# Normalized x of chunks 1 to 3 turned by VectorE instead of TensorE, between two tiles of 8 KB, with x loaded sooner

## The chip, the cores and the metric

The kernel runs on one core of one Trainium2 chip. The core has a matrix engine (TensorE, PE in the profile), a vector engine (VectorE, DVE), a scalar engine (ScalarE, ACT), a general engine (GpSimd, POOL) and a queue engine (SyncE, SP) that here issues DMAs. The metric is the time of one execution on the device in microseconds. The kernel before takes 844.69 us (median of three runs, 844.31 to 852.22).

## The reference

The input x has 2048 tokens of 512 values, all arithmetic is in fp32. One normalized copy of x feeds two branches, whose product is added to x:

```
xn = (x - mean) / sqrt(var + 1e-5)              # per token
qkv = xn @ wqkv                                 # 512 -> 3 x 32 heads x 16
p = softmax(q k^T * 16**-0.5, keys 0..255 behind the query)
s = (p v, heads side by side) @ wo
b = (silu(xn @ w_gate) * (xn @ w_up)) @ w_down  # hidden width 1792
out = x + s * silu(b)
```

A matrix product on TensorE sums over the partitions. So xn, which is loaded with tokens on the partitions, is needed turned: its 512 values on the partitions (four pieces k of 128) and tokens along the columns.

## The kernel before

**Chunks and units.** The tokens go in four chunks of 512. For each chunk TensorE runs dense units: projections to q and k (`Proj`, tiles "a"), gate and up (`GateUp`, "g" and "u"), values ("vp"), down ("d"), and the output projection of the chunk before ("s"). All of them go through line 619. For accuracy every operand is a sum of a high part and a low part, and a product is three matmuls: high x high, high x low, low x high. Names ending in h and l are these parts: xh, xl of the turned x, wh, wl of the weights. ScalarE rounds the high part, and another engine subtracts it to get the low one.

**Two halves.** The 128 rows of the array are used as two halves of 64 rows. A unit's sum runs first over the rows of the lower half (r = 0), and, some steps later, over those of the upper half (r = 1), into the same bank of PSUM. While the upper half still works on one unit, the lower half is on the next. Between the two stands a hand-over: a small copy on VectorE (tile "ho", line 616) that reads the bank after the lower half's last matmul. Four banks serve the dense units and four serve attention.

**Attention.** 32 units of four heads (eight per chunk). For each, scores are made once for the row maximum (b, line 1347; jk on VectorE, line 1355) and once transposed for the exponentials (c, line 1475; p on ScalarE), then probabilities times values (pv, line 1523). Every unit's maxima are turned by four small VectorE transposes (mr, line 1377). These short matmuls are placed between the dense ones. Queries, keys and results pass through DRAM.

**Normalizing and turning x.** `load_x` (line 259) fetches four tiles of 128 tokens by 512 values, takes mean and variance on VectorE, the inverse root partly on GpSimd, and scales in place (two tiles by VectorE, two by GpSimd). `xt_turn` (line 628) then turns one piece k: four tiles times two halves make eight TensorE transposes (xp, line 639) into two banks, ScalarE copies each bank to xh (line 657), VectorE subtracts to get xl (line 654). Four visits per chunk. Chunk 0 is turned in a similar way from its own code at the start, and once more by `xt_turn`.

**What sets the order.** All instructions are written out by a planner that runs while the program is built. It keeps a clock for each half of TensorE and each engine, with assumed costs. Work for the other engines waits in a queue per engine with an urgency; the most urgent that can go is emitted as soon as the engine is free in the plan. On TensorE, the half with the earlier clock gets the next matmul; a half whose inputs, weights or bank are not there by the plan gets none, and the other half goes on alone:

```
able = [r for r in range(2) if times[r] is not None and times[r] <= max(clock[r], now[0])]
...
r = min(able, key=lambda r: clock[r])
```

Attention and turning are started by due times, in units of `PACE` of dense work, less `LEAD`. The load of chunk c is due at 8c - `LXD`, its turning at 8c - `XTD`. So a change of a constant can move every instruction. The emitted order is fixed; on the chip each engine works through its instructions in that order and waits where a semaphore isn't there.

**Tiles.** 14 tiles of 128 x 512 values (`slots`) serve x, the evacuated q and k, hidden values, attention results and the x that is added at the end. `take` gets one and `give` returns it. `SURE` is the margin after which a tile that GpSimd reads counts as free, `MG` the urgency of the weights' low parts.

Of the kernel before, what the change touches and what calls it, by code (L numbers as in the profile page):

```python
# [9 lines left out]
F32 = mybir.dt.float32  # L10
F32R = mybir.dt.float32r
BF16 = mybir.dt.bfloat16
AF = mybir.ActivationFunctionType
ALU = mybir.AluOpType
# [3 lines left out]
P = 128  # L18
# [6 lines left out]
KC = D // P  # L25
# [14 lines left out]
NSL = 14  # L40
# [2 lines left out]
OPEN = 11  # L43
PRESS = 1.0
MS = 5.5
MG = 4.0
SPARE = 2
LAG = 7
MW = 80
SURE = 0.598  # L50
MTC = 0.85
CO = 1.075
MSG = 0.0
QKG = 1.0
LXD = 5.0
XTD = 3.5
WSL = 0.778
VDUE = 0.75

# [2 lines left out]
PRIO = -0.5  # L62
MM = 0.2315
PACE = 17.6
LEAD = 1.04
OUT = 2.4
STEP = 0.05
LAND = 3.5
# [4 lines left out]
def tile_window_attention_swiglu_gate(  # L73
# [12 lines left out]
    nc = tc.nc  # L86
    ctx.enter_context(tc.manual_schedule())
    pers = ctx.enter_context(tc.tile_pool(name="pers", bufs=1))
# [17 lines left out]
    def f32(ap):  # L106
        return ap.bitcast(F32)
# [38 lines left out]
    def timer(t, fn, *a):  # L146
        seq[0] += 1
        heapq.heappush(timers, (t, seq[0], fn, a))
# [20 lines left out]
                    again = True  # L169


    slots = [f"sl{i}" for i in range(NSL)]
    held = {}

    def take(name, shape=(P, 512), dtype=F32):
        assert slots, name
        tag = slots.pop(0)
        t = pers.tile(list(shape), dtype, name=name, tag=tag, bufs=1)
        held[id(t)] = (t, tag)
        return t  # L180

    def give(t):
        slots.append(held.pop(id(t))[1])

    def room(n):
        return lambda: len(slots) >= n
# [72 lines left out]
    def load_x(c):  # L259
        mv = pers.tile([P, 4, 2], F32, name=f"mv{c}", tag="mv")  # L260
        ve, rs, tm, nm = (
            pers.tile([P, 4], F32, name=f"{n}{c}", tag=n) for n in ("ve", "rs", "tm", "nm")
        )
        left = [4]


        def stats(i):
            st = sb(f"st{c}_{i}", [P, 6], F32, "st", 2)
            nc.vector.bn_stats(st, xt[c, i])
            nc.vector.bn_aggr(mv[:, i, :], st)  # L270

        small, se = nc.gpsimd, "G"

        def eps():
            small.tensor_scalar(ve, mv[:, :, 1], EPS, None, op0=ALU.add)
            small.tensor_scalar(nm, mv[:, :, 0], -1.0, None, op0=ALU.mult)

        def roots(r=rs):

            i32 = mybir.dt.int32  # L280
            nc.vector.tensor_scalar(tm.bitcast(i32), ve.bitcast(i32), 1, None, op0=ALU.logical_shift_right)
            nc.vector.tensor_scalar(  # L282
                r.bitcast(i32), tm.bitcast(i32), -1, 0x5F3759DF, op0=ALU.mult, op1=ALU.add
            )

        def newton():
            for _ in range(3):
                small.tensor_tensor(tm, rs, rs, op=ALU.mult)
                small.tensor_tensor(tm, tm, ve, op=ALU.mult)
                small.tensor_scalar(tm, tm, -0.5, 1.5, op0=ALU.mult, op1=ALU.add)  # L290
                small.tensor_tensor(rs, tm, rs, op=ALU.mult)

        def scale(i):
            (nc.gpsimd if i % 2 else nc.vector).tensor_scalar(
                xt[c, i], xt[c, i], nm[:, i : i + 1], rs[:, i : i + 1], op0=ALU.add, op1=ALU.mult
            )

        sl = 3.0

        def fetch(i):  # L300
            xt[c, i] = take(f"xt{c}_{i}")
            move(xt[c, i], x[c * TC + i * P : c * TC + (i + 1) * P, :])

        def after_stats(t):
            left[0] -= 1
            if left[0] == 0:
                do(se, t, 0.25, eps, after_eps, sl)

        def after_eps(t):
            do("V", t, 0.3, roots, after_rec, sl)  # L310

        def after_rec(t):
            do(se, t, 2.4, newton, after_newton, sl)

        def after_newton(t):
            for i in range(4):
                e = "G" if i % 2 else "V"
                do(e, t, 1.1 if e == "G" else 0.55, lambda i=i: scale(i), lambda t, i=i: scaled(t, i), sl + 0.3 * i)

        def scaled(t, i):  # L320
            normed[c, i] = t

        for i in range(4):
            dma(now[0], lambda i=i: fetch(i), lambda t, i=i: do("V", t, 0.8, lambda: stats(i), after_stats, sl),
                slack=0.1 * i, can=room(5 - i + SPARE))

    turns = {}
    cready = {}
# [299 lines left out]
    def xt_turn(c, k):  # L628
        left = [2]
        for r in range(2):  # L630
            pb, tag = bank(rb_free, f"xp{c}_{k}_{r}")
            src = pb[:, :256].rearrange("p (t n) -> p t n", n=R)
            hi, lo = (
                xn[c % 2][s][:, k, :].rearrange("p (t r n) -> p t r n", r=2, n=R)[:, :, r, :]
                for s in range(2)
            )

            def go(t, r=r, pb=pb):
                nc.tensor.matmul(  # L639
                    pb[:, R * t : R * t + R], xt[c, t][half(r), k * P : (k + 1) * P],  # L640
                    ident[half(r), half(r)], is_transpose=True, start=True, stop=True,
                )

            def done(t, tag=tag):
                rb_free[tag] = t
                left[0] -= 1
                if left[0] == 0:
                    xready[c, k] = t
                    if k == KC - 1:
                        for i in range(4):  # L650
                            give(xt.pop((c, i)))

            def low(src=src, hi=hi, lo=lo):
                nc.vector.tensor_tensor(lo, src, f32(hi), op=ALU.subtract)

            def finished(t, src=src, hi=hi, low=low, done=done):
                do("S", t, 0.3, lambda: nc.scalar.activation(hi, src, AF.Copy),
                   lambda t: do("V", t, 0.35, low, done, 0.3), 0.3)

            for t in range(4):  # L660
                extra[r].append((128, lambda t=t, go=go: go(t), finished if t == 3 else None))

    PAIRS = ((0, 0), (0, 1), (1, 0))

# [921 lines left out]
    def plan_attention():  # L1586
        for u in range(NU):
            c = u // NG
            if u:
                marks.append((u - 1 + 0.3, load_qk, (u,)))  # L1590
            for n in range(8):
                streams[0].append((u + 0.02 + 0.1 * n, max_ready, max_pair, (u, n // 4, n % 4)))
            ne = 3
            for n in range(2 * ne):
                streams[1].append((u + CO + 0.13 * n, prob_ready, prob_pair, (u, n // 2, n % 2)))
            streams[1].append((u + 1.89, pv_ready, pv_visit, (u,)))
        for c in range(NCH):
            if c:
                marks.append((8 * c - LXD, load_x, (c,)))
            for k in range(KC):  # L1600
                due = 8 * c - XTD + 0.25 * k if c else -9.0
                streams[2].append((due, xt_ready, xt_turn, (c, k)))
        for s in streams:
            s.reverse()
        marks.sort(key=lambda m: -m[0])
# [259 lines left out]
```

## Time and profile before

| | before |
|---|---|
| median of three runs | 844.69 us |
| the profiled execution | 844.67 us |
| its span | 842.6 us |
| granted clock of TensorE | 0.999 |
| TensorE busy | 834.6 us (99%) |
| VectorE busy | 525.5 us (62%) |
| ScalarE busy | 488.4 us (58%) |
| GpSimd busy | 629.6 us (75%) |

The span runs from the first to the last instruction of the program; the execution's time is 2.07 us longer. PE is the matmuls, PEld the loading of their stationary operand, which overlaps them. Matmuls of the two halves run side by side and are pipelined: one of 512 columns shows about 0.39 us, and the pace is read from the distance of the starts. In the lists of groups, a row has the line, engine, operation, tiles (out<-in), shapes, count, then busy time in us and mean ns of one, then the idle time before them and what ended it. In the lists of waits, a row has who waited for whom, the us in total, the number of times and the longest. The chain of waits is the work that ended last, followed back from the end.

### The profile page before, as it was taken

To read this page: it belongs to the slowest core of one execution; us is meant where nothing else is said; L and a number is where in the kernel's file an instruction comes from. 1 tells how busy PE (TensorE), PEld (TensorE's weight loads), DVE (VectorE), ACT (ScalarE), POOL (GpSimd) and SP (SyncE) were. 2 spreads that over 40 slices of the span, in tenths; PEclk is the share of its full clock that TensorE was granted. 3 is DMA by queue.
4 is the path that set the end of the run, shared out by engine and by line. 5 is a ranking of instruction groups with operands and counts; after the bars stand their busy time and mean duration, and the time that the engine had idled before them with its cause. 6 is when DMAs were issued, how large, how long until landed. Compare 5 with 4: busy or idle time off the path is not lost.

```text
span 842.6 us, 26272 instructions
## 1 busy us (share of the span) xinstructions
PE 834.6 (99%) x9962; PEld 752.8 (89%) x9962; DVE 525.5 (62%) x1772; ACT 488.4 (58%) x950; POOL 629.6 (75%) x887
## 2 busy tenths in 40 slices
PE   8999999999999999999999999999999999999997
PEld 8999978988889999888988999889888889989887
DVE  4247786766756757667646976666646676645235
ACT  6545656665665566564666657655467565556531
POOL 6567695878867888677977897867688877888771
PEclk9999999999999999999999999999999999999999
DMA  6586866876678966467768968664878576764442
GB/s 171 159 211 146 198 138 156 185 180 162 160 192 198 266 163 160 117 173 169 169 157 208 230 150 193 150 168 117 203 176 210 113 195 178 173 154 103 115 107 73
DMA packets 67143, 139.98 MB, mean 166 GB/s; under 512 B 14710, under 2 KB 17654, under 8 KB 67016
## 3 DMA queue, kind: packets, MB, share of 16 engines
q1 hardware_dynamic: 66552, 137.64, 67.0%
q8 instruction: 79, 1.29, 0.7%
q10 hardware_dynamic: 464, 0.66, 0.3%
q14 instruction: 48, 0.39, 0.2%
HBM read 107.68 MB, written 29.62 MB: 163 GB/s over the span
## 4 chain that ended last, share of the span: by engine, by line
PE 97%; DVE 1%; DMA 1%; issue 0%; POOL 0%; DVEq 0%; SPq 0%; POOLq 0%
PE u L619 20%; PE d L619 19%; PE g L619 19%; PE a L619 9%; PE pv L1523 8%; PE c L1475 6%; PE s L619 6%; PE vp L619 6%; PE b L1347 4%; DMA xt<-x 1%; PE xp L639 0%; PE xp L457 0%; DVE jk L1355 0%; DVE rs L282 0%; DVE s L1196 0%
## 5 line engine op out<-in xcount | busy, mean ns | idle before, releaser
L579 POOL TENSOR_TENSOR wl<-wr,wh 128x512 fp32r<-128x512 f32 (+1 forms) x239 | 305.4, 1291 | 63.2 <-ACT wh L574 61.0
L1355 DVE CUSTOM_DVE_ANT_0 jk<-b,maskb 128x384 bf16<-128x384 f32 (+2 forms) x512 | 271.2, 530 | 93.2 <-PE b L1347 45.2
L1435 ACT ACTIVATE p<-c 128x512 f32<-128x512 f32 (+2 forms) x384 | 196.3, 572 | 77.9 <-PE c L1475 72.6
L619 PE MATMUL d<-wh,hh 64*128 64x512 f32 x896 | 227.8, 393 | 0.0
L574 ACT ACTIVATE wh<-wr 128x512 fp32r<-128x512 f32 (+1 forms) x239 | 145.1, 627 | 34.8 <-PE d L619 13.8
L619 PE MATMUL g<-xh,wh 64*128 64x512 f32 x448 | 152.9, 393 | 0.0
L619 PE MATMUL g<-xh,wl 64*128 64x512 f32 x448 | 152.8, 393 | 0.0
L619 PE MATMUL u<-xh,wl 64*128 64x512 f32 x448 | 152.1, 392 | 0.0
L619 PE MATMUL u<-xl,wh 64*128 64x512 f32 x448 | 152.1, 392 | 0.0
L619 PE MATMUL g<-xl,wh 64*128 64x512 f32 x448 | 151.9, 393 | 0.0
L619 PE MATMUL u<-xh,wh 64*128 64x512 f32 x448 | 151.8, 393 | 0.0
L619 PE MATMUL d<-wl,hh 64*128 64x512 f32 x448 | 145.7, 392 | 0.0
L619 PEld LDWEIGHTS d<-wh,hh 64*128 64x128 f32 x896 | 136.1, 185 | 6.2
L1447 POOL TENSOR_SCALAR_AFFINE_SELECT p<-p 128x256 f32<-128x256 f32 x256 | 102.4, 412 | 47.1 <-ACT p L1435 46.5
L1347 PE MATMUL b<-k,q 48*128 48x384 f32 (+2 forms) x512 | 111.1, 329 | 0.4 <-DVE m L1355 0.4
L774 POOL TENSOR_TENSOR hh<-h,hh 128x512 fp32r<-128x512 f32 x56 | 72.6, 1296 | 46.8 <-ACT hh L770 44.6
L1451 POOL TENSOR_SCALAR_AFFINE_SELECT p<-p 128x256 f32<-128x256 f32 x224 | 91.7, 411 | 17.8 <-ACT p L1435 16.1
L619 PE MATMUL a<-xh,wh 64*128 64x512 f32 x256 | 93.9, 392 | 0.0
L1475 PE MATMUL c<-q,k 49*128 49x128 f32 (+2 forms) x704 | 93.8, 299 | 0.0
L619 PE MATMUL a<-xl,wh 64*128 64x512 f32 x256 | 93.0, 392 | 0.0
L619 PE MATMUL a<-xh,wl 64*128 64x512 f32 x256 | 93.0, 392 | 0.0
L1475 PEld LDWEIGHTS c<-q,k 49*128 49x128 f32 x704 | 82.9, 186 | 5.1 <-DVE m L1355 0.2
(116 smaller groups left out, 1884.7 us busy)
## 6 DMA issues: line engine op xcount, KB each, us to landing
wr<-wgu SPq DMA_DIRECT2D x112, 256.0 KB
wr<-wdn SPq DMA_DIRECT2D x48, 256.0 KB
k<-qkd SPq DMA_DIRECT2D x48, 192.0 KB
wr<-wqk SPq DMA_DIRECT2D x32, 256.0 KB
qkd<-qkh SPq DMA_DIRECT2D x32, 256.0 KB
qkd<-qkl SPq DMA_DIRECT2D x32, 256.0 KB
q<-qkd SPq DMA_DIRECT2D x64, 128.0 KB
od<-ev SPq DMA_DIRECT2D x32, 256.0 KB
```

Of the source, the lines that this page charges most:

```text
L574: nc.scalar.activation(wtile[j, h][0][pr, a - 512 * h : b - 512 * h], raw[pr, a:b], AF.Copy)
L579: nc.gpsimd.tensor_tensor(lo, raw[pr, a:b], f32(hi), op=ALU.subtract)
L619: return nc.tensor.matmul(pb, a, b, start=first, stop=last, skip_group_check=True)
L774: nc.gpsimd.tensor_tensor(hl[:, 1, :], self.h, f32(hl[:, 0, :]), op=ALU.subtract)
L1347: nc.tensor.matmul(pb[:, :n], qs[u % 3][r : r + 48, p, qb * P : (qb + 1) * P], ks[u % 3][r : r + 48, p, lo : lo + n], start=True, stop=True,)
L1355: nc.vector.tensor_tensor_reduce(junk[:, :n], pb[:, :n], maskb[:, 3 * P - n :], 1.0, -3.0e38, ALU.add, ALU.max, m[:, col : col + 1],)
L1435: nc.scalar.activation(t[:, h, :], pc[:, :n], AF.Exp, scale=DH ** -0.5)
L1447: nc.gpsimd.affine_select(s, s, [[0, 2], [1, P]], ALU.is_ge, 0.0, base=0, channel_multiplier=-1)
L1451: nc.gpsimd.affine_select(s, s, [[0, 2], [-1, P]], ALU.is_gt, 0.0, base=0, channel_multiplier=1)
L1475: nc.tensor.matmul(pc[:, at0 : at0 + w], ks[u % 3][r : r + 49, p, k0 : k0 + P], qs[u % 3][r : r + 49, p, qb * P : qb * P + w], start=(i == ...
L1523: nc.tensor.matmul(pbs[r][0][32 * j : 32 * j + 32, q0:q1], vt[half(r), (4 * c + kb) % VT, VW * (4 * g + j) : VW * (4 * g + j) + 32], t[hal ...
```

## The change

The turning of chunks 1 to 3 leaves TensorE. x is loaded into one tile of 128 x 4 x 512 values (`wides[0]`, 8 KB per partition), each token tile in a fourth of it. After scaling, 16 instructions on VectorE turn it into a second such tile (`wides[1]`). One instruction takes 32 partitions (a block b of tokens) and the columns of one group f of values, 512 columns in all, turns its blocks of 32 x 32 and writes to 32 partitions. When all 16 are done, ScalarE copies each of four pieces k to xh, and GpSimd subtracts to get xl. Before, the subtraction was VectorE's, and the copies and subtractions went by half pieces from PSUM.

The two tiles are eight of the 14 tiles of `slots`: while a chunk doesn't need them, their fourths are given out as ordinary tiles, after the six others. `hold_wide` collects the four fourths before the load, or before the turning; `give_wide` returns them. Constants of the planner change as well: loads and turning are due sooner, `LEAD` shifts all due times, `SURE` is shorter, the `SPARE` tile kept back is one instead of two, and `MG` grows. Chunk 0 stays as it was.

```diff
-MG = 4.0
-SPARE = 2
+MG = 4.572
+SPARE = 1
...
-SURE = 0.598
+SURE = 0.243
...
-LXD = 5.0
-XTD = 3.5
+LXD = 5.8
+XSL = 0.5
+XDS = 1.0
+XDD = 3.3
+XDU = 1.5
+XTD = 4.4
...
-LEAD = 1.04
+LEAD = 1.173
...
-    slots = [f"sl{i}" for i in range(NSL)]
+    slots = [f"sl{i}" for i in range(NSL - 8)]
+    wides = [pers.tile([P, 4, 512], F32, name=f"wide{i}") for i in range(2)]
+    wide = wides[0]
+    slots += range(8)
...
-            xt[c, i] = take(f"xt{c}_{i}")
+            xt[c, i] = wide[:, i]
...
+    def hold_wide(n, c, then):
+        for i in range(4 * n, 4 * n + 4):
+            if i in slots:
+                slots.remove(i)
+                wide_held[n].append(i)
+        if len(wide_held[n]) == 4:
+            then(c)
+        else:
+            timer(now[0] + 0.3, hold_wide, n, c, then)
...
+    def x_wait(c):
+        if any((c, t) not in normed for t in range(4)):
+            timer(now[0] + 0.3, x_wait, c)
+            return
+        hold_wide(1, c, x_blocks)
+
+    def x_blocks(c):
+        left = [16, KC]
+
+        def blocks(b, f):
+            q = slice(32 * b, 32 * b + 32)
+            src = wide[q].rearrange("q t (k f d) -> q f t k d", f=4, d=32)[:, f]
+            dst = wides[1][32 * f : 32 * f + 32].rearrange("d k (t b q) -> d b t k q", b=4, q=32)[:, b]
+            nc.vector.transpose(dst, src)
+
+        def turned(at):
+            left[0] -= 1
+            if left[0] == 0:
+                timer(at, give_wide, 0)
+                for k in range(KC):
+                    do("S", at, 0.52, lambda k=k: high(k), lambda t, k=k: after_high(t, k), XSL + 0.3 * k, lambda: c in x_free)
+
+        def high(k):
+            nc.scalar.activation(xn[c % 2][0][:, k, :], wides[1][:, k], AF.Copy)
+
+        def low(k):
+            nc.gpsimd.tensor_tensor(xn[c % 2][1][:, k, :], wides[1][:, k], f32(xn[c % 2][0][:, k, :]), op=ALU.subtract)
...
+        for n in range(16):
+            do("V", max(now[0], at), 0.72, lambda n=n: blocks(n // 4, n % 4), turned,
+               lambda n=n: now[0] + n * 0.01 + (XDS if work[0] / PACE - LEAD < 8 * c - XDD else -XDU))
...
-                marks.append((8 * c - LXD, load_x, (c,)))
-            for k in range(KC):
-                due = 8 * c - XTD + 0.25 * k if c else -9.0
-                streams[2].append((due, xt_ready, xt_turn, (c, k)))
+                marks.append((8 * c - LXD, hold_wide, (0, c, load_x)))
+                marks.append((8 * c - XTD, x_wait, (c,)))
+            for k in range(KC if not c else 0):
+                streams[2].append((-9.0, xt_ready, xt_turn, (c, k)))
```

In the rows of the order below, as in the profile, a number follows each name. Units are named by chunk and place: u2_5 is up, chunk 2, hidden block 5; d2_0_1 is down, chunk 2, first quarter, token tile 1. Line 619 of before is line 651 after, 616 is 648, 1355 is 1426. A row of the two halves can be told by its unit: at the places shown, the lower half is one unit or more ahead.

More of the change, by code (lines that the diff above doesn't have):

```diff
@@ L177, in take @@
         tag = slots.pop(0)
-        t = pers.tile(list(shape), dtype, name=name, tag=tag, bufs=1)
+        if isinstance(tag, int):
+            t = wides[tag // 4][:, tag % 4]
+            if len(shape) == 3:
+                t = t.rearrange("p (a n) -> p a n", a=shape[1])
+            elif shape[1] < 512:
+                t = t[:, : shape[1]]
+            t = t if dtype == F32 else t.bitcast(dtype)
+        else:
+            t = pers.tile(list(shape), dtype, name=name, tag=tag, bufs=1)
         held[id(t)] = (t, tag)
@@ L182, in give @@
     def give(t):
-        slots.append(held.pop(id(t))[1])
+        tag = held.pop(id(t))[1]
+        slots.insert(len(slots) if isinstance(tag, int) else sum(not isinstance(o, int) for o in slots), tag)
     def room(n):
@@ L324, in load_x, with give_wide @@
             dma(now[0], lambda i=i: fetch(i), lambda t, i=i: do("V", t, 0.8, lambda: stats(i), after_stats, sl),
-                slack=0.1 * i, can=room(5 - i + SPARE))
+                slack=0.1 * i)
+    wide_held = [[], []]
+    def hold_wide(n, c, then):
[5 more added lines that the diff above has]
+            then(c)
+        else:
+            timer(now[0] + 0.3, hold_wide, n, c, then)
+    def give_wide(n):
+        slots.extend(wide_held[n])
+        wide_held[n].clear()
     turns = {}
@@ L661, in xt_turn, with after_high @@
                 extra[r].append((128, lambda t=t, go=go: go(t), finished if t == 3 else None))
+    def x_wait(c):
[20 more added lines that the diff above has]
+            nc.gpsimd.tensor_tensor(xn[c % 2][1][:, k, :], wides[1][:, k], f32(xn[c % 2][0][:, k, :]), op=ALU.subtract)
+            left[1] -= 1
+            if left[1] == 0:
+                timer(free_at["G"] + SURE, give_wide, 1)
+        def after_high(t, k):
+            do("G", t, 1.24, lambda: low(k), lambda t: xready.__setitem__((c, k), t), XSL + 0.3 * k)
+        at = max(normed[c, t] for t in range(4))
+        for n in range(16):
+            do("V", max(now[0], at), 0.72, lambda n=n: blocks(n // 4, n % 4), turned,
+               lambda n=n: now[0] + n * 0.01 + (XDS if work[0] / PACE - LEAD < 8 * c - XDD else -XDU))
     PAIRS = ((0, 0), (0, 1), (1, 0))
```

## The prediction

> **What bounds the kernel now.** I read the page first: span, busy shares, the chain that ended last.
>
> ```profile
> span 842.6 us, 26272 instructions
> ...
> PE 834.6 (99%) x9962; PEld 752.8 (89%) x9962; DVE 525.5 (62%) x1772; ACT 488.4 (58%) x950; POOL 629.6 (75%) x887
> ...
> PE 97%; DVE 1%; DMA 1%; issue 0%; POOL 0%; DVEq 0%; SPq 0%; POOLq 0%
> ```
>
> TensorE is busy 99% of the span and carries 97% of the chain. A busy PE could still be one that waits inside, so the next view is the list of what TensorE waited for, complete:
>
> ```profile
> PE warm L257 <- DVE warm L252: 1.1, 1, 1.1
> PE xp L457 <- DVE xt L359: 1.0, 1, 1.0
> PE xp L457 <- issue: 0.5, 1, 0.5
> PE b L1347 <- DVE m L1355: 0.4, 1, 0.4
> PE s L619 <- DVE ho L616: 0.3, 1, 0.3
> ```
>
> The first three are the opening, which the change leaves. In the other 820 us TensorE waits 0.7 us (0.4 + 0.3). So no other engine sets the time: it is the number of TensorE instructions and how well the two 64-row halves of the array overlap. The chain by line gives the share of the transposes that the change removes, and the source view of L639 (from 100 us on) how many belong to chunks 1 to 3:
>
> ```profile
> by line: PE u L619 19.5%; PE d L619 19.3%; PE g L619 18.8%; PE a L619 9.3%; PE pv L1523 8.3%; PE c L1475 5.9%; PE s L619 5.8%; PE vp L619 5.7%; PE b L1347 4.0%; DMA xt<-x 0.6%; PE xp L639 0.5%; issue 0.4%; PE xp L457 0.2%; DVE jk L1355 0.2%
> ...
> L639 PE MATMUL xp<-ident,xt x96: 213/222/225, 132.6 to 518.3; 64*128 64x64 f32 x96
> ```
>
> **Removed: 96 transposes on TensorE.** 0.5% of 842.6 us is 4.2 us for all 128 of L639; 96/128 of it is 3.2 us. The same from one visit (8 transposes), in the timeline:
>
> ```profile
> 312.27 0.40 PE L619 MATMUL g<-xh,wh 64*128 64x512 f32 x1
> 312.40 0.40 PE L619 MATMUL g<-xl,wh 64*128 64x512 f32 x1
> 312.51 0.41 PE L639 MATMUL xp<-ident,xt 64*128 64x64 f32 x6
> 312.73 0.48 PE L619 MATMUL g<-xl,wh 64*128 64x512 f32 x1
> 312.76 0.29 PE L639 MATMUL xp<-ident,xt 64*128 64x64 f32 x2
> 312.86 0.58 PE L619 MATMUL g<-xh,wl 64*128 64x512 f32 x2
> ...
> 313.17 0.49 PE L619 MATMUL g<-xh,wh 64*128 64x512 f32 x2
> 313.40 0.49 PE L619 MATMUL g<-xl,wh 64*128 64x512 f32 x2
> 313.64 0.49 PE L619 MATMUL g<-xh,wl 64*128 64x512 f32 x2
> ```
>
> Undisturbed, a pair of dense matmuls (one per half) comes every 0.23 us (313.17, 313.40, 313.64). Across the visit each half goes from 312.27 to 312.73, and from 312.40 to 312.86: 0.46 us, so a visit costs 0.23 us, and 12 visits 2.8 us. Both ends stand: 2.8 to 3.2. I take **-3.0 us**, all on the path.
>
> **Moved: the order on TensorE.** The constants and the new holding of tiles make another order. Dense matmuls of 512 columns alternate between the halves, so that two share a step. Counted over the order after the opening, one is followed directly by another of its own half 7 times before and 48 times after. One such place is in chunk 2, on TensorE, where u2_5 ends on the upper half and the lower half is already on d2_0. Before, they take turns:
>
> ```order
> L619 MATMUL d2_0_1_9697<-wh72_1_9289,hh2_1_8325 128x512
> L619 MATMUL u2_5_9542<-xh0_79,wl72_1_9290 128x512
> L619 MATMUL d2_0_1_9697<-wh73_0_9320,hh2_2_8889 128x512
> L619 MATMUL u2_5_9542<-xh0_79,wh72_1_9289 128x512
> L619 MATMUL d2_0_1_9697<-wl73_0_9321,hh2_2_8889 128x512
> L619 MATMUL u2_5_9542<-xl0_80,wh72_1_9289 128x512
> ```
>
> The same place after:
>
> ```order
> L651 MATMUL d2_0_1_9586<-wh73_0_9203,hh2_2_8810 128x512
> L651 MATMUL u2_5_9424<-xl0_82,wh72_1_9186 128x512
> L651 MATMUL u2_5_9424<-xh0_81,wl72_1_9187 128x512
> L651 MATMUL u2_5_9424<-xh0_81,wh72_1_9186 128x512
> L651 MATMUL u2_5_9424<-xl0_82,wh72_1_9186 128x512
> L651 MATMUL d2_0_2_9623<-wh72_0_9172,hh2_0_7807 128x512
> ```
>
> Four of the upper half now stand in a row, and the lower half gets nothing meanwhile. The reason lies in the program: while a chunk is turned, both 8 KB tiles are held, and of 14 free tiles 6 are left, so an evacuation of PSUM finds its tile later and the next unit its bank later. What a lone half costs shows in the tail of before, in matmuls of 256 columns:
>
> ```profile
> 835.61 0.39 PE L619 MATMUL s<-wh,xl 64*128 64x256 f32 x2
> 835.73 0.39 PE L619 MATMUL s<-wh,xh 64*128 64x256 f32 x2
> ...
> 837.15 0.28 PE L619 MATMUL s<-wl,xh 64*128 64x256 f32 x1
> 837.27 0.28 PE L619 MATMUL s<-wh,xl 64*128 64x256 f32 x1
> ```
>
> Two per 0.12 us with both halves, one per 0.12 with one. So a matmul of 512 alone takes the 0.23 that two share: 0.115 us lost. In runs of three or more of one half, 4 neighbours became 31: 27 x 0.115 = 3.1 us. The other 14 are single swaps, which may cost 0.115 each (1.6 us) or nothing, if the half that goes twice had fallen behind. So 3.1 to 4.7 by this reckoning; I take the middle, **+3.9 us**, on the path. The short matmuls of attention are counted at nothing: c is followed by its own half 24 times less, b 36 times more, and at 0.08 us each (a b of 384 columns by the 0.23 for 512: 0.17 for two) that is +1 us at most.
>
> **Added on VectorE: 48 transposes (L708); removed: 24 subtractions (L654).** Prices from these groups and one stretch of the timeline:
>
> ```profile
> L1377 DVE STREAM_TRANSPOSE mr<-m 32x32 f32<-32x32 f32 x128 | 25.5, 199 | 1.9
> L269 DVE BATCH_NORM_STATS2 st<-xt 128x6 f32<-128x512 f32 x12 | 8.2, 686 | 0.1
> L654 DVE TENSOR_TENSOR xl<-xp,xh 128x256 fp32r<-128x256 f32 x32 | 12.5, 418 | 6.0 <-ACT xh L657 5.9
> L657 ACT ACTIVATE xh<-xp 128x256 fp32r<-128x256 f32 x32 | 10.4, 385 | 6.3 <-PE xp L639 6.3
> L770 ACT ACTIVATE hh<-h 128x512 fp32r<-128x512 f32 x56 | 35.4, 633 | 52.1 <-DVE h L766 52.1
> L774 POOL TENSOR_TENSOR hh<-h,hh 128x512 fp32r<-128x512 f32 x56 | 72.6, 1296 | 46.8 <-ACT hh L770 44.6
> ...
> 293.11 0.81 DVE L1377 STREAM_TRANSPOSE mr<-m 32x32 f32<-32x32 f32 x4
> ```
>
> No row shows a transpose of 512 columns. One of 32 takes 0.20; 256 more columns cost 0.686 - 0.418 = 0.27 us, so 480 more some 0.50: 0.70 us. Lower end: 0.69, as other work on 512 columns. Upper end: each 32 columns at what four now take (0.81 / 4 = 0.20), 16 x 0.20 = 3.2 us. I take 0.70, nearest to the rows with 512 columns. VectorE gets 48 x 0.70 - 24 x 0.418 = +23.6 us, some 8 per chunk.
>
> **ScalarE and GpSimd.** ScalarE: 12 copies of 0.633 for 24 of 0.385: -1.6 us. GpSimd: 12 subtractions of 1.296: +15.6 us, 5.2 per chunk. What covers all this is idle time where the work falls (before's turning of the three chunks lies at 132 to 155, 312 to 334 and 498 to 518 us; the new copies come at its end):
>
> ```profile
> core 0: us, PE busy (x) PEld busy (x) DVE busy (x) ACT busy (x) POOL busy (x), PEclk, DMA share, GB/s
> 125.00:150.00 25.00, 25.00 (x338) 19.67 (x336) 15.79 (x57) 15.32 (x34) 15.58 (x21) 1.00 0.65 166
> 325.00:350.00 25.00, 25.00 (x349) 23.32 (x341) 18.07 (x61) 13.43 (x26) 18.61 (x27) 1.00 0.51 118
> 515.00:540.00 25.00, 25.00 (x314) 21.91 (x312) 15.44 (x53) 18.18 (x36) 19.84 (x30) 1.00 0.69 161
> ```
>
> VectorE is idle 9.2, 6.9 and 9.6 us of 25, GpSimd 9.4, 6.4 and 5.2. The added 8 and 5.2 fit, barely in two places; hence **0** on the path. Without the cover, chunk c's first projections would wait for xl, and everything behind them on TensorE.
>
> **Waits added.** The order on VectorE shows what now stands behind the transposes. Before, chunk 1, behind the copies "ho" (L616, the hand-over without which a unit's upper half can't start):
>
> ```order
> L711 TENSOR_TENSOR qkl0_7_2502<-a0_7_2331,qkh0_7_2491 128x512
> L616 COPY ho_2517<-u0_9_2453 80x1
> L756 SCALAR_TENSOR_TENSOR h0_9_2556<-h0_9_2556,g0_9_2393 128x512
> L616 COPY ho_2578<-g0_10_2514 80x1
> L1355 ISA jk4_3_2_2599,m0_70<-b4_3_2_2587,maskb_69 128x384
> ```
>
> After:
>
> ```order
> L708 STREAM_TRANSPOSE wide1_69<-wide0_68 32x4x4x32 x3
> L648 COPY ho_2504<-g0_9_2417 80x1
> L782 TENSOR_TENSOR qkl0_6_2510<-a0_6_2304,qkh0_6_2473 128x512
> L708 STREAM_TRANSPOSE wide1_69<-wide0_68 32x4x4x32 x3
> L782 TENSOR_TENSOR qkl0_7_2564<-a0_7_2360,qkh0_7_2525 128x512
> L648 COPY ho_2573<-u0_9_2486 80x1
> ```
>
> Hand-overs now stand behind up to four transposes (2.8 us). The first transpose of a chunk also waits for GpSimd's scaling of x and, in chunk 2, for stores out of the second tile; behind it in VectorE's queue stand jk, which frees banks, and ho. Each is planned to be over by then; price 0, up to some 1 us per chunk. SyncE's queue keeps its transfers; the four loads of x go out sooner (LXD 5.8 units ahead of their chunk for 5.0), past other loads and stores, and TensorE waits for no DMA now (its list has none): 0. SURE returns tiles 0.36 us sooner, MG orders the weight splits: no wait of TensorE hangs on them now; 0.
>
> **Sum.** Profiled execution 844.67 us (span 842.6, 2.07 around it), 0.02 under the median of 844.69. -3.0 + 3.9 + 0 = +0.9: **845.6 us**.
>
> **A rule against the change.** TensorE does a quarter of a chunk's turning in a 0.23 us visit; VectorE needs four instructions, 2.8 us. The Trainium skill, "VectorE: DVE Perf Modes", Rules for kernel authors, says to transpose 128x128 on TensorE where the result may go to PSUM, as here. This trace agrees on the engine's cost and shows what the rule leaves out: TensorE's 0.23 us is on the path, VectorE's 2.8 us need not be. The same page (The three transpose paths) gives VectorE 311 ns for a 128x128 of bf16; by that a chunk's 16 blocks would take an estimated 5.0 us instead of 11.2, which with VectorE off the path leaves the sum at 845.6.
>
> **Rivals.**
> - *The order costs nothing*: a half that stands alone was due to wait anyway, and the two waits of 0.7 us go as well. 844.67 - 3.0 = 841.7, down to 844.67 - 3.2 - 0.7 = 840.8. For it: TensorE hardly waits now. Against: the idle half is fixed in the order, whether or not its reason comes true. 0.27.
> - *VectorE comes onto the path* (what the rule above would lead to): at 1.2 us per transpose (twice the slope per column) runs of three hold VectorE 3.6 us, 1.5 longer than at 0.7; the ho behind is late by that, and TensorE runs one half at half pace: 0.75 us. Ten runs of two to four stand in the order: 7.5 us, 853.1: slower. It decides from about 0.9 us per transpose. For it: no row has such an instruction. Against: both nearest rows. 0.13. At the upper end of 3.2 us, VectorE needs 40 us more per chunk where 10 are idle: 3 x 30 = 90 us more, 936; 0.01, outside the range.
> - *GpSimd late*: 5.2 us more beside idle 5.2 in chunk 3; xl then comes late and the projections of that chunk wait, 1 to 4 us: 847 to 850. 0.08.
> - That it doesn't do what it says is out: the order has the 48 transposes.
>
> **Chances.** The forecast, 843 to 848: 0.51; the rivals as above. Likeliest: 845.6. The range leaves out the lowest edge, and most of the slow case: 841 to 850. A run here can tell 1% (8.4 us) from no change. Faster by over 1% needs under 836.2: all removals and every wait of TensorE come to 3.2 + 0.7, so 0.02. Slower by over 1% (853.1) needs VectorE on the path: half its case and the end, 0.07. Within: 0.91.
>
> **What would show it.** TensorE's wait list still under some 5 us, its instructions 96 fewer, and in u2_5 of chunk 2 steps of 0.23 with one matmul each: the order's cost. L708 at 0.7 us: VectorE's price right; at 1.2 with waits "PE <- DVE ho": the second rival. A wait of "PE a <- POOL xl": the third. A time under 842 with alone-standing halves that pass at 0.115 each would make the order term wrong.

## The result, and the profile after

The changed kernel takes 841.04 us (median of 14 runs, 840.55 to 841.66), the kernel before 844.83 us beside it (14 runs). The ratio is 0.9949, with a 95% interval of 0.9935 to 0.9962: 0.5% faster, where 0.1% slower was forecast. The profiled execution of the changed kernel took 841.51 us, 3.16 less than before's 844.67.

The head of its profile page, and the share of each engine in the chain that ended last:

```profile
span 839.7 us, 26047 instructions
...
PE 832.1 (99%) x9866; PEld 748.0 (89%) x9866; DVE 548.9 (65%) x1796; ACT 488.3 (58%) x938; POOL 642.1 (76%) x899
...
PE 97%; DVE 1%; POOL 1%; DMA 1%; issue 0%; ACT 0%; SPq 0%; DVEq 0%
```

TensorE has 96 instructions fewer (9962 before) and is the bound as before. VectorE has 23.4 us more work, GpSimd 12.5. What TensorE waited for, complete:

```profile
PE warm L273 <- DVE warm L268: 1.1, 1, 1.1
PE xp L489 <- issue: 0.9, 1, 0.9
PE xp L489 <- DVE xt L391: 0.8, 1, 0.8
PE s L651 <- DVE ho L648: 0.3, 1, 0.3
PE c L1546 <- DVE ho L648: 0.3, 1, 0.3
```

Behind the opening it waits 0.6 us, where it was 0.7. The moved work, by groups:

```profile
L708 DVE STREAM_TRANSPOSE wide<-wide 32x512 f32<-32x512 f32 x48 | 33.7, 703 | 1.1
L721 POOL TENSOR_TENSOR xl<-wide,xh 128x512 fp32r<-128x512 f32 x12 | 15.3, 1303 | 1.9 <-ACT xh L718 1.9
```

Now the place that the prediction quoted from the order, in chunk 2, where four matmuls of u2_5 stand in a row in the program. TensorE's timeline there (start, duration, instruction):

```profile
513.40 0.39 PE L651 MATMUL u<-xl,wh 64*128 64x512 f32 x1
513.40 0.39 PE L651 MATMUL d<-wh,hh 64*128 64x512 f32 x1
513.63 0.39 PE L651 MATMUL u<-xh,wl 64*128 64x512 f32 x1
513.64 0.39 PE L651 MATMUL d<-wh,hh 64*128 64x512 f32 x1
513.86 0.39 PE L651 MATMUL u<-xh,wh 64*128 64x512 f32 x1
513.87 0.39 PE L651 MATMUL d<-wl,hh 64*128 64x512 f32 x1
514.09 0.39 PE L651 MATMUL u<-xl,wh 64*128 64x512 f32 x1
514.10 0.39 PE L651 MATMUL d<-wh,hh 64*128 64x512 f32 x1
```

One u and one d start in every 0.23 us. The row of four costs nothing: d's matmuls on the lower half start beside those of u that stand ahead of them in the program.

Where TensorE's time went, worked out from the traces: each step from the start of one matmul to the start of the next is given to the matmul that began it, and the steps are summed. Dense matmuls and those of attention stand in one row, since they share steps. A "lone step" is a dense matmul of 512 columns with no other start within 0.185 us on either side, between 20 and 800 us: one half works alone there. The opening ends at the first start after 14 us.

| us | before | after | difference |
|---|---|---|---|
| transposes of x (xp) | 4.46 | 1.20 | -3.26 |
| dense and attention | 819.12 | 820.14 | +1.02 |
| from the last matmul to the end | 5.02 | 4.30 | -0.72 |
| opening | 14.05 | 14.06 | +0.01 |
| span | 842.65 | 839.70 | -2.95 |
| lone steps | 4 | 12 | +8 |

The removal came out at 3.3 us, just above the 2.8 to 3.2 forecast. The order costs 1.0 us, not 3.9.

### The profile page after: what moved, and what is told of

It is laid out like the page before. It is cut to its first block, busy times and chain, and to the rows that moved or that the text cites. A ratio compares the mean times of both kernels' runs of the same rounds, so it can differ in the third digit from the quotient of the medians.

```text
span 839.7 us, 26047 instructions
## 1 busy us (share of the span) xinstructions
PE 832.1 (99%) x9866; PEld 748.0 (89%) x9866; DVE 548.9 (65%) x1796; ACT 488.3 (58%) x938; POOL 642.1 (76%) x899
## 4 chain that ended last, share of the span: by engine, by line
PE 97%; DVE 1%; POOL 1%; DMA 1%; issue 0%; ACT 0%; SPq 0%; DVEq 0%
PE u L651 19%; PE d L651 19%; PE g L651 18%; PE a L651 11%; PE pv L1594 9%; PE c L1546 6%; PE vp L651 6%; PE s L651 5%; PE b L1418 4%; DMA xt<-x 1%; DVE jk L1426 0%; PE xp L489 0%; POOL p L1518 0%; PE xp L671 0%; DVE s L1267 0%
## 5 line engine op out<-in xcount | busy, mean ns | idle before, releaser
L651 PE MATMUL g<-xh,wl 64*128 64x512 f32 x448 | 165.1, 392 | 0.0
L651 PE MATMUL u<-xh,wh 64*128 64x512 f32 x448 | 164.3, 392 | 0.0
L651 PE MATMUL u<-xh,wl 64*128 64x512 f32 x448 | 164.1, 392 | 0.0
L651 PE MATMUL u<-xl,wh 64*128 64x512 f32 x448 | 163.9, 392 | 0.0
L651 PE MATMUL g<-xh,wh 64*128 64x512 f32 x448 | 163.4, 392 | 0.0
L651 PE MATMUL g<-xl,wh 64*128 64x512 f32 x448 | 162.9, 392 | 0.0
L651 PE MATMUL d<-wl,hh 64*128 64x512 f32 x448 | 158.1, 392 | 0.0
L651 PEld LDWEIGHTS d<-wh,hh 64*128 64x128 f32 x896 | 144.8, 185 | 7.1 <-issue 0.6
L1418 PE MATMUL b<-k,q 48*128 48x384 f32 (+2 forms) x512 | 116.8, 328 | 0.0
L1522 POOL TENSOR_SCALAR_AFFINE_SELECT p<-p 128x256 f32<-128x256 f32 x224 | 90.7, 408 | 15.6 <-ACT p L1506 14.0
L845 POOL TENSOR_TENSOR hh<-h,hh 128x512 fp32r<-128x512 f32 x52 | 67.4, 1296 | 38.7 <-ACT hh L841 38.7
```

The costliest lines, as they stand in the source:

```text
L651: return nc.tensor.matmul(pb, a, b, start=first, stop=last, skip_group_check=True)
L845: nc.gpsimd.tensor_tensor(hl[:, 1, :], self.h, f32(hl[:, 0, :]), op=ALU.subtract)
L1418: nc.tensor.matmul(pb[:, :n], qs[u % 3][r : r + 48, p, qb * P : (qb + 1) * P], ks[u % 3][r : r + 48, p, lo : lo + n], start=True, stop=True,)
L1522: nc.gpsimd.affine_select(s, s, [[0, 2], [-1, P]], ALU.is_gt, 0.0, base=0, channel_multiplier=1)
```

## The experiments

Two theories at the start. **In order**: a matmul starts after those ahead of it in the program, so a row of one half leaves the other half empty, 0.115 us a neighbour, as the prediction had it. **Passing**: a half's matmuls start past those of the other half that still wait, and only a long row costs.

**1. Runs of one half alone.** A kernel of its own, which computes nothing of the reference: 24 matmuls of 512 columns for each half, each half into a bank of its own, written in runs of n:

```diff
+    while left[0] or left[1]:
+        m = min(n, left[h])
+        left[h] -= m
+        yield from [h] * m
+        h = 1 - h
```

Then pairs with a single run of n more on one half and later one on the other.

> A kernel of its own that computes nothing of the reference: 24 matmuls of 512 columns on each half of TensorE, written in runs of 1, 2, 3, 4, 5, 6, 8 and 12 of one half (tiles runa to runh); then 24 pairs that take turns, with one run of n more of the upper half after the eighth pair and n more of the lower after the sixteenth, n = 0, 1, 2, 3, 4, 5, 6, 8 (oncea to onceh). A step of a pair is 0.23 us. Theory 'in order' (the prediction's): a matmul does not start before those written ahead of it, so runs of 1 and 2 take 24 x 0.23 = 5.5 us, runs of 3 take 7.4, of 4 8.3, of 6 9.2, of 12 10.1; one run of n costs 0.46 n us in the two places, 1.8 us for n = 4. Theory 'halves pass each other': a half goes on past the other's waiting matmuls, up to some depth; runs up to that depth take 5.5 us, and a single run of n up to it costs only the added work, 0.23 n; over the depth it goes towards the first theory's numbers.

For 48 matmuls, from the first start to the last: 6.09 us in runs of 2, 6.09 (3), 6.15 (4), 6.20 (5 and 6), 6.94 (8), 8.54 (12). Up to runs of six, each half's own 24 take 5.3 to 5.6 us; the rest is that the lower half starts 0.7 to 0.9 us sooner. A single run of up to 3 more cost 0.23 to 0.25 us for each added pair, as two in turn do; from there on 0.41 to 0.45, as two alone. Two stretches are left out: runs of 1 (6.93 us) began with 0.42 us a pair up to 11.0 us, and the one with no more (7.25) waited for VectorE after its first matmul. "In order" asked for 7.4 at runs of 3 and falls. The start of the stretch with runs of three (tile runcl on the lower half, runcu on the upper; the program has three l, three u, three l and so on):

```profile
22.53 0.97 PE L61 MATMUL runcl<-mv,wt 64*128 64x512 f32 x3 [0.25 <-ACT y L71]
23.25 0.49 PE L61 MATMUL runcu<-mv,wt 64*128 64x512 f32 x1
23.34 0.41 PE L61 MATMUL runcl<-mv,wt 64*128 64x512 f32 x1
23.59 0.39 PE L61 MATMUL runcu<-mv,wt 64*128 64x512 f32 x1
```

The fourth of the lower half starts at 23.34. The second and third of the upper half stand ahead of it in the program and start at 23.59 and later. One figure covers both series: over all their stretches, no matmul started with more than three of the other half's ahead of it still to start, and from runs of four on some had three. With the matmul of the pair ahead of it, a single run of n more is n + 1 long, so it costs from its fifth matmul on; in steady runs both halves give three each, and runs of six are nearly free. The lone steps of a kernel would then be the sum, over runs that stand alone, of their length less four, and where runs follow on runs, of their length less six.

The Trainium skill states the contrary ("TensorE: Matmul & The Clock Gate", Part 3, The mechanism): "MATMULs are pc-monotone in start AND end — strict FIFO, no reordering." These starts, for two halves of 64 rows, do not agree with it: 23.34 comes before 23.59.

**2. The same in the real kernel.** The kernel before, with the planner made to stay on a half for N matmuls (3 here, 8 in the second run) and its clocks made to let a half run ahead by as many steps:

```diff
+        at = max(clock[r], front[0] - 3 * 0.24)
+        front[0] = max(front[0], at)
...
+            if last[0] in able and last[1] % 3 and clock[last[0]] - clock[1 - last[0]] < 3 * 0.24:
+                r = last[0]
+            last[:] = [r, last[1] + 1 if r == last[0] else 1]
```

> The kernel before with the matmuls of each half of TensorE written in runs of about three in the program, the same matmuls otherwise (3421 neighbours of one half, 2993 of them in runs of three and more). Halves in the order of the program, as the prediction had it: 2993 x 0.115 = +344 us, so about 1190 us. Halves that pass each other over runs of this length, as in the small kernel (runs of 3 and 4 took 6.09 and 6.15 us where runs of 2 took 6.09): within 1% of before, 843 to 853 us. In between, 900 to 1100, would mean that a half passes only some of the time in the real kernel, because what it waits for is also behind in the order.

> As the run with runs of three, but runs of six to twelve (4313 neighbours of one half). In program order: about 1330 us. By the small kernel, where runs of 8 cost 0.14 us a run and runs of 12 cost 0.61 us a run: 105 x 0.14 + 51 x 0.61 + some 15 for the runs of 7 and the odd long ones = some 60 us, so 880 to 960 us. If there is no limit on how far a half passes the other: 845 to 855.

Runs of three: 874.46 us, ratio 1.0354 (1.0339 to 1.037). Of the 344 us of "in order" 30 came, but 843 to 853 was missed as well. By the sums of steps the dense matmuls take 641.6 us as in before (641.7); the matmuls of scores, b and c, take 133.9 for 105.5. So dense halves pass each other in runs of three as in the small kernel. Why the short score matmuls lose when they are placed among runs was not settled. Runs of eight: 1033.79 us (ratio 1.2241, 1.2196 to 1.2285). That is more than the 880 to 960 of "passing" with its limit, and less than the 1330 of "in order"; without any limit it would have been about 850. From 20 us to the end there are 71 lone steps with runs of three, and 850 with runs of eight. Length less six, over the runs of the two programs, gives 0 and 722. So the count comes near, and the time does not: 189 us over before are 0.22 us for each lone step, not 0.115.

**3. The removal alone.** Before, with the transposes of chunks 1 to 3 left out and the copy and subtraction reading the unturned x, so that chunks 1 to 3 are not the reference's:

```diff
-            src = pb[:, :256].rearrange("p (t n) -> p t n", n=R)
+            src = (xt[c, k][:, 256 * r : 256 * r + 256] if c else pb[:, :256]).rearrange("p (t n) -> p t n", n=R)
...
+                if c:
+                    return
```

> The kernel before without the 96 transposes of chunks 1 to 3 on TensorE and nothing put in their place: the order of everything else is the same, and the copies and subtractions read x as loaded, not turned (the result of chunks 1 to 3 is not the reference's). Theory 'the gain is the removal': 2.8 to 3.2 us under the kernel before, 841.6 to 842.0, about what the changed kernel takes. Rival 'the gain is in the order and constants, the transposes were as good as hidden': within 1 us of the kernel before.

844.8 us, ratio 1.0019 (0.9994 to 1.0044): no gain, against the expectation. But the edit made something slower. The subtraction, now from SBUF, by groups:

```profile
L656 DVE TENSOR_TENSOR xl<-xt,xh 128x256 fp32r<-128x256 f32 x24 | 20.8, 891 | 2.8 <-ACT xh L659 2.8
```

0.891 us on the mean (0.41 to 1.51) in place of 0.418 from PSUM, and TensorE waited 1.6 us for VectorE's maxima, where it was 0.4. By steps, xp fell by 3.25 us and dense and attention grew by 3.1. The run can't decide; the next one keeps PSUM as the source.

**4. Three quarters of the removal.** Of each visit's eight transposes two stay, and the copies read their 64 columns four times; one token tile stands for four, so chunks 1 to 3 are again not the reference's:

```diff
+            if c:
+                src = pb[:, :R].unsqueeze(1).to_broadcast([P, 4, R])
...
+                if c and t < 3:
+                    return
+                if c:
+                    t = 0
```

> The kernel before with two of the eight transposes left in each visit of chunks 1 to 3 (72 of 96 gone); copies and subtractions still read PSUM, the same 64 columns four times, so that the result of chunks 1 to 3 is not the reference's. The order is the kernel before's. It takes back what was wrong with the run without any transpose, in which the subtractions read two tiles of SBUF and took 0.89 us for 0.42. Theory 'the gain is the removal': three quarters of the 3.26 us between starts that went with the 96, 2.4 us: 842.2 to 842.6. Rival 'the visits fill time that is lost anyway': within 0.5 us of the kernel before, 844.3 or more.

843.18 us beside 844.56, ratio 0.9981 (0.9957 to 1.0004); the profiled span is 840.6 for 842.6. By steps xp gives 2.69 of its 4.46 back, 72/96 of the 3.26 being 2.4; dense and attention take 0.7 again. The median is 1.4 us lower, not the 2.0 to 2.4 expected, and the interval just reaches 1: the run points to a gain from the removal, of less than its whole price, and does not show it.

**5. Constants and mechanism apart.** Before with the six constants of the change, and after with four of the old ones:

```diff
-MG = 4.572
+MG = 4.0
-SPARE = 1
+SPARE = 2
-SURE = 0.243
+SURE = 0.598
-LEAD = 1.173
+LEAD = 1.04
```

> The kernel before with the six changed constants (MG 4.572, SPARE 1, SURE 0.243, LEAD 1.173, LXD 5.8, XTD 4.4), still turning on TensorE. Theory 'the gain is the removal': within 1 us of the kernel before, 844 to 846. Rival 'the constants gain': 841 to 842.

> The changed kernel with MG 4.0, SPARE 2, SURE 0.598, LEAD 1.04 as before; turning by VectorE and x loaded sooner stay. Theory 'the gain is the removal': within 1 us of the changed kernel, 840.5 to 842. Rival 'the constants gain': 844 or more.

Before with new constants: 844.3 us, ratio 0.9994 (0.9968 to 1.0021); dense and attention take 819.80 us, 0.7 more than in before, and from the last matmul to the end it is 0.5 less. After with old ones: 844.65, ratio 1.0022 (1.0 to 1.0044), and not the 840.5 to 842 expected. The transposes are gone there too (1.20 us), but dense and attention take 822.48 us, 2.34 more than in after, with 22 lone steps, and 4.87 us lie behind the last matmul, 0.57 more. So the whole gain of the change can go in the order. That left open whether it is the runs of one half, or something else that the constants move.

**6. Other constants.** Three versions of after with MG, SURE, WSL and LEAD moved, chosen by the number of neighbours beyond the second of a run in their orders:

> The changed kernel with four constants moved (MG 4.834, SURE 0.094, WSL 0.844, LEAD 1.162): its order holds 6 neighbours of one half beyond the second of a run, the changed kernel's 9. If only such neighbours cost: 841.0 - 3 x 0.115 = 840.7 us, and 6 to 9 lone steps of dense matmuls. If constants also move time by waits or by where the score matmuls fall: 840 to 845 us with those few lone steps.

> The changed kernel with MG 4.181, SURE 0.374, WSL 0.649, LEAD 1.142: 8 neighbours beyond the second of a run. If only such neighbours cost: 840.9 us, and 8 to 11 lone steps. If something else moves too: 840 to 845 us.

> The changed kernel with MG 4.642, SURE 0.17, WSL 0.92, LEAD 1.247: 38 neighbours beyond the second of a run, in runs of up to ten. If only such neighbours cost: 841.0 + 29 x 0.115 = 844.4 us, and some 38 lone steps. By the prediction's account (every neighbour in runs of three and more at 0.115: 63 of its 82, the changed kernel 26 of its 48) 845.3 us. If halves pass each other without limit: 841.0 us and no more than 12 lone steps.

| kernel | neighbours beyond the second | lone steps | dense and attention, us | median, us |
|---|---|---|---|---|
| before | 0 | 4 | 819.12 | 844.83 |
| before, new constants | 5 | 7 | 819.80 | 844.30 |
| after, constants "6" | 6 | 9 | 819.47 | 840.49 |
| after, constants "8" | 8 | 13 | 820.38 | 841.43 |
| after | 9 | 12 | 820.14 | 841.04 |
| after, old constants | 22 | 22 | 822.48 | 844.65 |
| after, constants "38" | 38 | 49 | 826.80 | 848.44 |

A neighbour beyond the second of a run is length less three. This count tells the lone steps from the program alone, 0 to 11 short; the small kernel's length less four gives 0, 3, 3, 5, 3, 16 and 28, which is 4 to 21 short, so in the real kernel a run costs somewhat sooner; why was not settled. The time follows the lone steps, and more steeply than the 0.115 us of the count: between after and "38" dense and attention grow by 6.66 us for 37 steps, 0.18 each. "38" was expected at 844.4, or at 845.3 by the prediction's own count (of neighbours in runs of three and more its order holds 68, not 63, and that of after 31, not 26; the difference is the same), and took 848.44. Part of the loss is thus beside the lone steps or weighs more than half a step; which was not settled. That lone steps cause the loss, rather than go along with it, is argued: the constants move other things too. One run of "38" in TensorE's timeline:

```profile
348.45 0.39 PE L651 MATMUL g<-xl,wh 64*128 64x512 f32 x1
348.68 0.39 PE L651 MATMUL g<-xh,wl 64*128 64x512 f32 x1
348.91 0.39 PE L651 MATMUL g<-xh,wh 64*128 64x512 f32 x1
349.15 0.39 PE L651 MATMUL g<-xl,wh 64*128 64x512 f32 x1
349.38 0.39 PE L651 MATMUL g<-xh,wl 64*128 64x512 f32 x1
```

One matmul per 0.23 us: this is what the prediction expected 31 times over in the changed kernel. Constants "6" make the fastest kernel of all, 840.49 us (ratio to before 0.995, 0.9935 to 0.9965), but its interval holds the changed kernel's ratio: no version is shown to beat it.

**7. What covers VectorE and GpSimd.** The prediction let idle time cover the moved work. How much cover is left? After with each transposition done twice, and after with each of GpSimd's twelve subtractions done twice:

```diff
             nc.vector.transpose(dst, src)
+            nc.vector.transpose(dst, src)
```

> The changed kernel with every one of the 48 VectorE transposes written twice in its place: 33.7 us more of VectorE, the order else the same. Theory 'they lie beside TensorE's work, with room': within 1 us of the changed kernel, 840.5 to 842. The prediction's second rival, 'runs of transposes hold up the hand-overs': at two times 0.70 us, 7 us or more, 848 and up, with waits of TensorE for the copies ho.

> The changed kernel with the 12 GpSimd subtractions of the turned x written twice: 15.5 us more of GpSimd in the stretches where it has least room. Theory 'there is room': within 1 us of the changed kernel. The prediction's third rival, 'GpSimd late': 1 to 4 us more, 842 to 845, with TensorE waiting for xl.

870.23 us (ratio 1.0286, 1.025 to 1.0321) for 33.7 us more of VectorE, which is then busy 67%, and 858.25 us (1.0144, 1.0106 to 1.0181) for 15.5 us more of GpSimd. The added time goes almost whole to the end: 29.2 and 17.2 us, some 5 of them in each case through a lower granted clock (last section). TensorE's longest waits beyond the opening, VectorE's case first, then GpSimd's:

```profile
PE b L1419 <- DVE m L1427: 6.1, 6, 2.6
PE c L1547 <- DVE m L1427: 3.3, 8, 0.7
PE g L651 <- DVE ho L648: 2.7, 2, 1.8
PE u L651 <- DVE ho L648: 2.4, 1, 2.4
```

```profile
PE pv L1595 <- POOL p L1519: 7.7, 4, 2.7
...
PE pv L1595 <- POOL p L1523: 0.7, 1, 0.7
```

What stands behind the transpositions on VectorE (maxima, hand-overs) and behind the subtractions on GpSimd (masks of p) is late, and TensorE's next instruction hangs on it. Waits for hand-overs, as the second rival had them, are among them; waits for xl, as the third had them, are not. Waits and clock make 21 of the 29.6 us by which the profiled span grew, and 13.5 of 15.6; the rest was not assigned. The shares of the whole span (65% and 76% in after) don't show this, the stretches do. After, in stretches of 25 us, those where the transpositions crowd (from 125, 310 and 495 us) and those where the subtractions start (at 150 to 154, 338 to 344 and 525 to 530 us; busy us and count for PE, PEld, VectorE, ScalarE and GpSimd, then TensorE's granted clock, the DMA share and GB/s):

```profile
125.00:150.00 25.00, 25.00 (x278) 21.68 (x276) 22.04 (x67) 13.89 (x29) 15.93 (x22) 1.00 0.74 178
150.00:175.00 25.00, 25.00 (x279) 22.96 (x278) 17.73 (x71) 14.02 (x30) 20.66 (x25) 1.00 0.61 158
...
310.00:335.00 25.00, 25.00 (x307) 22.75 (x305) 22.25 (x61) 15.42 (x29) 19.43 (x27) 1.00 0.85 171
335.00:360.00 25.00, 25.00 (x307) 22.89 (x305) 18.75 (x62) 16.08 (x31) 22.74 (x34) 1.00 0.53 120
...
495.00:520.00 25.00, 25.00 (x301) 22.35 (x299) 22.17 (x62) 13.81 (x28) 16.61 (x26) 1.00 0.83 200
520.00:545.00 25.00, 25.00 (x307) 22.60 (x305) 15.64 (x54) 17.29 (x34) 23.95 (x33) 1.00 0.46 101
```

VectorE is busy 22.0, 22.3 and 22.2 of 25 us in the first kind, and GpSimd 20.7 (from 150 us), 22.7 and 24.0 in the second: the change has used most of the cover up. If the 2.8 to 3.0 us of VectorE's idle time take up that much of the 11.2 us more per chunk, the other 8.3 make 25 us in three chunks, of the 29.6 by which the span grew (839.7 to 869.3). This is argued, not shown: in the same stretches of the doubled run VectorE is busy 22.1, 21.9 and 21.9 us, so it did not fill its idle time there. Next, the same two with the doubled time told to the planner:

```diff
-            do("V", max(now[0], at), 0.72, lambda n=n: blocks(n // 4, n % 4), turned,
+            do("V", max(now[0], at), 1.44, lambda n=n: blocks(n // 4, n % 4), turned,
```

> The changed kernel with every transposition on VectorE done twice, as in the run that took 870.2 us, but with 1.44 in place of 0.72 us as the planner's cost for the pair. If it is the plan that hides VectorE's time (the work that TensorE waits for is put ahead of the transpositions, and the transpositions start early enough): 842 to 850 us, the upper part because this order holds more and longer runs of one half. If VectorE's time itself binds although the engine is busy for 65% of the span: about 870 us again.

> The changed kernel with every one of GpSimd's 12 subtractions done twice, as in the run that took 858.3 us, but with 2.48 in place of 1.24 us as the planner's cost for the pair. If the plan hides GpSimd's time: 841 to 848 us. If GpSimd's time itself binds, busy for 78% of the span: about 858 us again.

GpSimd: 851.11 us (1.0061 to 1.0091), between the two theories. The waits on the masks are gone from the list, but the order now has 53 lone steps; 41 more than after at 0.18 make 7 of the 10 us. VectorE: 894.51 us (1.0573 to 1.0608), worse than unplanned. TensorE waits less (some 7 us in place of 16), but a lower granted clock costs some 22 us (last section), and 77 lone steps at the full clock, 65 more than in after, some 12 at 0.18. So this planner could move some of GpSimd's time out of the way, and none of VectorE's: unplanned work came back as waits, planned work as halves that go alone and a slower clock.

## Why the prediction was wrong

- **The bound** (TensorE's count of instructions and the overlap of its halves): right. Waits stayed at 0.6 us.
- **Removal, -3.0 (2.8 to 3.2)**: -3.26 in the traces, a little over the upper end. Taken away alone, three quarters of the transposes shortened the profiled span by 2.0 us and the median by 1.4, with an interval that holds no change.
- **Order, +3.9 (3.1 to 4.7)**: the step that failed. "One is followed directly by another of its own half 7 times before and 48 times after" was counted rightly, and what a lone half costs was read from the tail. But the program's order was taken for the order of starts. A half passes up to three matmuls of the other, so only long rows leave a half alone: of 41 more neighbours 9 lie beyond the second of a run, and 8 more lone steps were counted. Measured: +1.0. The price of 0.115 was, if anything, too low: 1.0 us for 8 lone steps is 0.13 each, and experiment 6 gives 0.18. The sum of the prediction with the measured terms: -3.26 + 1.02 - 0.72 + 0.01 = -2.95 us on the profiled span, and 0.2 less around it. Of the 4.1 us between 845.6 and the profiled 841.51 the order makes 2.9. The -0.72, between the last matmul and the end, the prediction did not have; other constants gave 4.13 to 4.87 us there, so they move it too.
- **VectorE, 0.70 us per transposition and +23.6 us**: 0.703 and +23.4. The rival at 1.2 us is out.
- **"Hidden, 0", since idle time in stretches of 25 us covers it, "barely"**: right, and the stretches are the view that shows it. VectorE is left with some 3 us idle in 25, and experiment 7 shows the price beyond: nearly the whole of what is added, in an order that is not made for it.
- **GpSimd +15.6, ScalarE -1.6**: the twelve subtractions took 1.303 each as priced; the engines' totals moved by +12.5 and -0.1, since other groups changed as well. Neither touched the end.
- **Waits added, 0**: right, 0.3 us of a hand-over.
- **The rival "the order costs nothing", 841.7**, came nearest in number, in part by luck: the order did cost 1.0 us, and the 0.7 us gained behind the last matmul, which the rival did not have, nearly make up for it. Its reason (a half that stands alone was due to wait anyway) is not what the traces show: in the row of four shown above neither half stood alone.

## What to carry to other kernels

Where two halves of TensorE work side by side, don't price an order by neighbours in the program: look in the timeline whether both halves start in each step, and count only rows longer than three or four; here each lone step then cost 0.13 to 0.22 us, more than the half step that it loses. A helper engine that is idle a third of the span may have nothing left where the work falls: read its idle time by stretches, and test it by doubling the added instruction. When a planner writes the order, a change's own gain and its constants must be tried together; here the constants without the change, and the change with four of the old constants, gave nothing that could be measured.

## What the runs showed of the hardware

- A matmul of one half of 64 rows started with up to three of the other half's ahead of it in the program still to start, and never with more (experiment 1).
- In the two doubled runs the granted clock fell three times each, in five of the six cases within 2 us after TensorE had stood idle for 2.2 to 2.7 us. GpSimd's doubled case, by stretches of 2 us (columns as above, the granted clock third from the end):

```profile
166.00:168.00 2.00, 0.00 (x0) 0.00 (x0) 0.00 (x0) 0.00 (x0) 2.00 (x3) 1.00 0.03 8
168.00:170.00 2.00, 1.87 (x36) 1.51 (x38) 0.55 (x1) 0.60 (x1) 2.00 (x3) 0.92 0.00 0
170.00:172.00 2.00, 2.00 (x12) 1.67 (x12) 1.46 (x6) 0.00 (x0) 2.00 (x3) 0.50 0.69 164
172.00:174.00 2.00, 2.00 (x16) 1.72 (x14) 0.62 (x2) 0.00 (x0) 1.05 (x1) 0.73 0.84 194
174.00:176.00 2.00, 2.00 (x22) 1.83 (x20) 1.82 (x9) 1.27 (x2) 1.21 (x1) 1.00 1.03 290
```

After the gap the clock stands at half for some 3.4 us, (2 x 0.08 + 2 x 0.5 + 2 x 0.27) / 0.5, so such a gap costs 1.7 us more than it lasts. Three such falls make some 5 us in each of the two doubled runs. A long gap isn't needed, though. In the planned VectorE case the clock stood at half for 10, 20 and 14 us, which is some 22 us lost, and the second time it fell with no idle stretch over 0.8 us in the 10 us before:

```profile
370.00:372.00 2.00, 1.22 (x11) 0.91 (x9) 1.55 (x5) 1.22 (x3) 0.06 (x1) 1.00 0.09 29
372.00:374.00 2.00, 1.66 (x10) 0.96 (x8) 1.92 (x5) 1.47 (x3) 2.00 (x4) 0.75 0.28 109
...
384.00:386.00 2.00, 2.00 (x6) 1.54 (x5) 0.00 (x0) 0.00 (x0) 0.16 (x1) 0.50 0.26 33
```

It came back only at some 393 us, after stretches with few matmuls (6 in 2 us here) in which TensorE shows as busy throughout. What amount of work keeps the clock up was not measured. The Trainium skill ("TensorE: Matmul & The Clock Gate", Part 1, What's actually happening) gives the half clock after at least one idle window of about 3.4 us, and the full one after a busy window as long. In the rows above, the return after 3.4 us in GpSimd's doubled case agrees; the fall came there after idle stretches of 0.7 and 2.2 us with 1.0 us of matmuls between, and in the planned VectorE case after none of that length.
- VectorE's subtraction of 128 x 256 took 0.42 us from PSUM and 0.41 to 1.51 us with both inputs in SBUF (experiment 3); what makes it vary is not shown.
